# Two-layer sink-attention MLP on one core: gate high parts and some weight low parts made by GpSimd in the first layer's first run, and two start-up steps placed ahead of the last attention output

## The chip, the cores and the metric

The kernel runs on one core of a Trainium2 chip. Its time is the device time of one execution in microseconds (us). The engines are named as the profile names them: PE (TensorE, matrix products), DVE (VectorE), ACT (ScalarE), POOL (GpSimd) and SP (SyncE, which here only issues transfers). Each engine works through its own list of instructions strictly in order; semaphores make one wait for another.

## The reference, cut to what matters

```
scores = q @ k^T / 8, kept only for 4 sink keys and the last 128 keys
a = softmax(scores);  x = (a @ v) as 1536 tokens x 512
h = x @ w_in (512 x 2048);   g = h - tanh(h);              y = g @ w_out (2048 x 512)
h = y @ w_in2;               g = h * clip(h + 3, 0, 6) / 6; out = g @ w_out2
```

The weights come as 64-bit floating point numbers; everything is computed to about 32-bit accuracy.

## The kernel before

**Tiles.** The tokens are worked in three chunks of 512. A chunk needs 64 groups: 32 for the first MLP (phase 0) and 32 for the second. A group is either one 128-row slice f of the hidden layer (12 products of 128x512 into one bank `ps_h`) or its contribution to the output (12 products into four banks `ps_y`). Each weight and each activation is held as a high part and a low part (`wh`, `wl`; `xh`, `xl`; `gh`, `gl`), so a product is three matmuls: high by high, high by low, low by high. Slice f's hidden group runs about two groups ahead of its output group (`LAG`).

**Weights.** Two groups make a pair; there are 32 pairs. In the first chunk (the first run through the weights) each pair p is decoded from its 64-bit words: `w_load` (SP, 1,024 KB into `raw`), `w_scale` (ACT L107, into `dec`), `w_exponent` (DVE L118), `w_sign` (ACT L127 and L131: the low word and the sign into `r`), `w_round` (DVE L137 adds `r` into `dec`), `w_keep` (SP writes the 32-bit result to DRAM), `w_split` (POOL L151 makes `wh`, DVE L154 makes `wl`). Later chunks read the kept words and split them with ACT (L153) and DVE. `raw`, `dec`, `wh` and `wl` have four buffers each, `r` has two.

**Gates.** For each slice f of phase 0, ACT L229 takes tanh of `ps_h` into `th`, DVE L231 subtracts, ACT L232 makes the high part `gh`, DVE L233 the low part `gl`. `th` has two buffers.

**Order.** Attention for the first chunk runs first (`startup`), with the decoding of the first pairs placed between its steps by the table `WARM` (tick, stage, pair). From then on `rest` writes MLP groups and the next chunk's attention in turn. The compiler's scheduler then sorts the instructions of each engine by a model of its own, except those marked to stay in program order (the loads and scales of pairs 0 to 5, the sign steps of pairs 0 to 3). So a small edit can reorder many instructions. The last attention output of the first chunk is copied to `xh` by ACT (L562) and to `xl` by DVE (L563).

Of the kernel before, what the change touches and what calls it, by code (L numbers as in the profile page):

```python
# [8 lines left out]
F32 = mybir.dt.float32  # L9
# [19 lines left out]
GROUPS = 64  # L29
PAIRS = GROUPS // 2  # L30
# [14 lines left out]
class Mlp:  # L45
# [97 lines left out]
    def w_split(self, p):  # L143
        if p >= self.n_pairs:
            return
        nc = self.nc
        src = self.dec.pop(p).bitcast(F32) if p < PAIRS else self.raw.pop(p)
        wh = self.spl_p.tile([128, 1024], F32R, tag="wh", name="wh")
        wl = self.spl_p.tile([128, 1024], F32R, tag="wl", name="wl")
        if p < PAIRS:  # L150
            nc.gpsimd.tensor_copy(out=wh, in_=src)  # L151
        else:
            nc.scalar.copy(out=wh, in_=src)  # L153
        nc.vector.tensor_sub(out=wl, in0=src, in1=wh.bitcast(F32))  # L154
        for i in range(2):
            self.spl[2 * p + i] = tuple(
                w[:, 512 * i:512 * (i + 1)].rearrange("p (k c) -> p k c", c=128) for w in (wh, wl)
            )
# [27 lines left out]
    def step(self, s):  # L186
        c, i = divmod(s, GROUPS)
        n = self.chunks[c]
        ph, l, f = self.order[i]
        self.w_step(s // 2, s % 2)  # L190
        kd, kf = self.kd, self.kf
        if l == 0:
            ah, al = (self.xh, self.xl) if ph == 0 else (self.yh, self.yl)
            wh, wl = self.spl.pop(s)
            ps = self.ps_h.tile([128, n], F32, tag="h", name="ps_h")
            for k in range(kd):
                self.mm3(ps, wh[:, k, :], wl[:, k, :], ah[:, k, 0:n], al[:, k, 0:n], k == 0, k == kd - 1)
            self.run_late()
            self.gate(ph, f, ps, n)
            return  # L200
        if f == 0:
            self.acc = [self.ps_y.tile([128, n], F32, tag="y", name="ps_y") for _ in range(kd)]
        if f < kf - LAG:
            wh, wl = self.spl.pop(s)
            gh, gl = self.g.pop(f)
            for d in range(kd):
                self.mm3(self.acc[d], wh[:, d, :], wl[:, d, :], gh, gl, f == 0, False)
            self.run_late()
            return
        self.run_late()  # L210
        if f < kf - 1:
            return
        back = {kf - 1: s, kf - 2: s - 1, kf - 3: s - 2}
        fs = sorted(back)
        ws = {j: self.spl.pop(back[j]) for j in fs}
        gs = {j: self.g.pop(j) for j in fs}
        for d in range(kd):
            for j in fs:
                self.mm3(self.acc[d], ws[j][0][:, d, :], ws[j][1][:, d, :], *gs[j], False, j == kf - 1)
            (self.keep_y if ph == 0 else self.store)(c, d, self.acc[d], n)  # L220

    def gate(self, ph, f, ps, n):
        nc = self.nc
        th = self.ev_p.tile([128, n], F32, tag="th", name="th")
        gh = self.g_p.tile([128, n], F32R, tag="gh", name="gh")
        gl = self.g_p.tile([128, n], F32R, tag="gl", name="gl")
        self.g[f] = (gh, gl)
        if ph == 0:
            nc.scalar.activation(out=th, in_=ps, func=ACTF.Tanh)  # L229
            u = th  # L230
            nc.vector.tensor_sub(out=u, in0=ps, in1=th)  # L231
            self.late.append(lambda: nc.scalar.copy(out=gh, in_=u))  # L232
            self.late.append(lambda: nc.vector.tensor_sub(out=gl, in0=u, in1=gh.bitcast(F32)))  # L233
        else:
            nc.scalar.activation(out=th, in_=ps, func=ACTF.Relu, bias=self.three)  # L235
            u = th
            nc.vector.scalar_tensor_tensor(out=u, in0=th, scalar=6.0, in1=ps, op0=ALU.min, op1=ALU.mult)  # L237
            self.late.append(lambda: nc.scalar.activation(out=gh, in_=u, func=ACTF.Copy, scale=1.0 / 6.0))
            self.late.append(lambda: nc.vector.scalar_tensor_tensor(
                out=gl, in0=u, scalar=1.0 / 6.0, in1=gh.bitcast(F32), op0=ALU.mult, op1=ALU.subtract  # L240
            ))
# [561 lines left out]
def banded(mlp, at):  # L803
# [12 lines left out]
    (5, "scale", 0), (5, "exponent", 0), (6, "sign", 0), (7, "round", 0),  # L816
    (8, "scale", 1), (8, "exponent", 1), (8, "keep", 0), (8, "split", 0), (9, "sign", 1),
    (10, "load", 4), (10, "round", 1), (11, "keep", 1), (11, "scale", 2), (12, "exponent", 2),
    (13, "sign", 2), (13, "load", 5), (13, "scale", 3), (13, "exponent", 3), (13, "scale", 4),
)  # L820


# [93 lines left out]
```

## Time and profile before

| what | value |
|---|---|
| median of 3 runs | 670.09 us (669.36 to 671.33) |
| the profiled execution | 672.98 us, span 671.3 us |
| PE busy over the span | 637.5 us (95%) |
| DVE, ACT, POOL busy | 399.8, 361.2, 102.4 us |

The span runs from the first to the last instruction; 1.7 us of the profiled execution lie around it. Busy shares are averages over very different stretches: the first 60 us are attention, up to about 240 us weights are still decoded, and from then on PE hardly ever waits. Times below are counted from the start of the span.

### The profile page before, as it was taken

The page shows a single profiled execution, that of the slowest core. Times are in us where ns is not written, and L with a number is a line of the kernel's source. Part 1 is how long each engine was busy: PE and PEld are TensorE (multiplying, and loading weights), DVE is VectorE, ACT ScalarE, POOL GpSimd, SP SyncE. Part 2 cuts the span into 40 slices and gives each one's busy share as a digit, 9 for nine tenths or more (in the row PEclk, how much of TensorE's full clock was granted, in tenths as well). Part 3 has the DMA queues.
Part 4 walks back from the last instruction along what each step waited for, and adds up shares of the span by engine and source line. Part 5 has one row for each costly group of instructions (what it writes and reads, how often), then busy time and mean ns, then how long its engine had stood idle before and what let it go on. Part 6 is the DMA issues. An engine that isn't in the chain of part 4 may idle for free.

```text
span 671.3 us, 8169 instructions
## 1 busy us (share of the span) xinstructions
PE 637.5 (95%) x2924; PEld 489.9 (73%) x2924; DVE 399.8 (60%) x721; ACT 361.2 (54%) x608; POOL 102.4 (15%) x108
## 2 busy tenths in 40 slices
PE   2976999999999999999999999999999999999995
PEld 2654777676777787887777777778788888888884
DVE  4776899987986844465545464544354444455431
ACT  3665899788878523354544464444344443454421
POOL 1222321434332440000112020201000000000000
PEclk9999899999999999999999999999999999999999
DMA  9897999877767822332322111122133313120001
GB/s 142 271 235 192 378 417 359 286 274 256 247 225 249 263 78 84 126 109 81 102 84 106 62 63 64 62 82 109 62 126 125 126 63 125 63 89 37 0 1 67
DMA packets 38898, 98.87 MB, mean 147 GB/s; under 512 B 17857, under 2 KB 25025, under 8 KB 30657
## 3 DMA queue, kind: packets, MB, share of 16 engines
q1 hardware_dynamic: 34624, 97.22, 43.9%
q10 hardware_dynamic: 4224, 1.05, 1.1%
q8 instruction: 25, 0.41, 0.3%
q14 instruction: 25, 0.20, 0.1%
HBM read 78.33 MB, written 19.92 MB: 146 GB/s over the span
## 4 chain that ended last, share of the span: by engine, by line
PE 77%; DVE 8%; ACT 7%; issue 2%; DMA 1%; SPq 0%; POOL 0%; DVEq 0%; ACTq 0%
PE ps_h L177 12%; PE ps_y L177 12%; PE ps_h L178 12%; PE ps_h L179 12%; PE ps_y L178 11%; PE ps_y L179 11%; PE ps_a L558 4%; PE ps_a L469 3%; DVE dec L137 2%; ACT r L127 2%; DVE dec L118 2%; ACT r L131 2%; ACT dec L107 1%; PE ps_a L519 1%; DVE wl L154 1%
## 5 line engine op out<-in xcount | busy, mean ns | idle before, releaser
L178 PE MATMUL ps_y<-gl,wh 128*128 128x512 f32 x384 | 151.3, 395 | 0.0
L179 PE MATMUL ps_y<-gh,wl 128*128 128x512 f32 x384 | 149.9, 391 | 0.0
L177 PE MATMUL ps_y<-gh,wh 128*128 128x512 f32 x384 | 143.8, 403 | 2.5 <-ACT gh L232 2.5
L154 DVE TENSOR_TENSOR wl<-raw,wh 128x1024 fp32r<-128x1024 f32 x64 | 79.2, 1238 | 57.5 <-ACT wh L153 56.2
L153 ACT CAST wh<-raw 128x1024 fp32r<-128x1024 f32 x64 | 67.2, 1050 | 47.8 <-PE ps_y L178 40.2
L177 PEld LDWEIGHTS ps_y<-gh,wh 128*128 128x128 f32 x384 | 71.9, 189 | 25.3 <-issue 6.4
L178 PEld LDWEIGHTS ps_y<-gl,wh 128*128 128x128 f32 x384 | 72.2, 188 | 17.1 <-issue 2.2
L179 PEld LDWEIGHTS ps_y<-gh,wl 128*128 128x128 f32 x384 | 72.1, 188 | 15.8 <-issue 0.5
L177 PE MATMUL ps_h<-xh,wh 128*128 128x512 f32 x192 | 77.5, 406 | 6.1 <-POOL wh L151 4.4
L177 PE MATMUL ps_h<-yh,wh 128*128 128x512 f32 x192 | 76.6, 403 | 1.8 <-ACT yh L245 1.8
L179 PE MATMUL ps_h<-xh,wl 128*128 128x512 f32 x192 | 76.6, 399 | 0.0
L178 PE MATMUL ps_h<-xl,wh 128*128 128x512 f32 x192 | 76.6, 399 | 0.0
L178 PE MATMUL ps_h<-yl,wh 128*128 128x512 f32 x192 | 76.1, 397 | 0.0
L179 PE MATMUL ps_h<-yh,wl 128*128 128x512 f32 x192 | 75.9, 396 | 0.0
L235 ACT ACTIVATE th<-ps_h,three 128x512 f32<-128x512 f32 x48 | 32.8, 685 | 68.9 <-PE ps_h L179 68.7
L237 DVE SCALAR_TENSOR_TENSOR th<-th,ps_h 128x512 f32<-128x512 f32 x48 | 32.9, 685 | 55.0 <-ACT th L235 54.8
L481 ACT ACTIVATE sc<-sc,mn 128x132 f32<-128x132 f32 x96 | 38.4, 402 | 43.0 <-DVE mn L477 32.7
L469 PE MATMUL ps_a<-qk 64*128 64x264 f32 (+1 forms) x192 | 45.3, 454 | 15.0 <-DVE delta L743 9.5
L151 POOL CAST wh<-dec 128x1024 fp32r<-128x1024 f32 x32 | 43.6, 1366 | 101.9 <-PE ps_y L178 49.6
L229 ACT ACTIVATE th<-ps_h 128x512 f32<-128x512 f32 x48 | 28.6, 596 | 47.1 <-PE ps_h L179 37.5
L231 DVE TENSOR_TENSOR th<-ps_h,th 128x512 f32<-128x512 f32 x48 | 32.9, 685 | 33.6 <-ACT th L229 33.3
L177 PEld LDWEIGHTS ps_h<-xh,wh 128*128 128x128 f32 x192 | 36.3, 190 | 18.3 <-POOL wh L151 5.3
(77 smaller groups left out, 872.7 us busy)
## 6 DMA issues: line engine op xcount, KB each, us to landing
raw<-in_w_dram SPq DMA_DIRECT2D x32, 1024.0 KB
raw<-keep SPq DMA_DIRECT2D x32, 1024.0 KB
keep<-dec SPq DMA_DIRECT2D x32, 512.0 KB
out_dram<-ob SPq DMA_DIRECT2D x12, 256.0 KB
qk<-in_qkv_dram SPq DMA_DIRECT2D x8, 325.0 KB
qk<-in_qkv_dram SPq DMA_DIRECT2D x8, 260.0 KB
qk<-in_qkv_dram SPq DMA_DIRECT2D x8, 195.0 KB
v<-in_qkv_dram SPq DMA_DIRECT2D x8, 160.0 KB
```

What stands on the lines that cost most here:

```text
L151: nc.gpsimd.tensor_copy(out=wh, in_=src)
L153: nc.scalar.copy(out=wh, in_=src)
L154: nc.vector.tensor_sub(out=wl, in0=src, in1=wh.bitcast(F32))
L177: mm(out=ps, lhsT=wh, rhs=ah, start=first, stop=False)
L178: mm(out=ps, lhsT=wh, rhs=al, start=False, stop=False)
L179: mm(out=ps, lhsT=wl, rhs=ah, start=False, stop=last)
L229: nc.scalar.activation(out=th, in_=ps, func=ACTF.Tanh)
L231: nc.vector.tensor_sub(out=u, in0=ps, in1=th)
L235: nc.scalar.activation(out=th, in_=ps, func=ACTF.Relu, bias=self.three)
L237: nc.vector.scalar_tensor_tensor(out=u, in0=th, scalar=6.0, in1=ps, op0=ALU.min, op1=ALU.mult)
L469: nc.tensor.matmul(out=ps[:, 0:w], lhsT=qk[:, e, 0:128], rhs=qk[:, first:e + 1, 128:KEYS], start=True, stop=True)
L481: ins = nc.scalar.activation(out=sc, in_=sc, func=ACTF.Exp, scale=-1.0, bias=mn, accum_out=s["sm"][:, a, i:i + 1])
```

## The change

In phase 0 of the first chunk (`s < 32`, pairs 0 to 15) the high part of each gate is made by POOL and no longer by ACT: 16 casts of 128x512. Of these pairs every fourth (3, 7, 11, 15) has its weight's high part made by ACT and its low part by POOL; before, POOL made the high and DVE the low part. And the start-up table has the sign step and scale steps of pairs 2 and 3 (with one load and one exponent step) one tick earlier, so that they are written ahead of the last attention output.

```
-        if p < PAIRS:
+        if p < PAIRS // 2 and p % 4 == 3:
+            nc.scalar.copy(out=wh, in_=src)
+        elif p < PAIRS:
             nc.gpsimd.tensor_copy(out=wh, in_=src)
         else:
             nc.scalar.copy(out=wh, in_=src)
-        nc.vector.tensor_sub(out=wl, in0=src, in1=wh.bitcast(F32))
+        low = nc.gpsimd if p < PAIRS // 2 and p % 4 == 3 else nc.vector
+        low.tensor_sub(out=wl, in0=src, in1=wh.bitcast(F32))
...
+        self.decoding = s < GROUPS // 2
         self.w_step(s // 2, s % 2)
...
-            self.late.append(lambda: nc.scalar.copy(out=gh, in_=u))
+            copy = nc.gpsimd.tensor_copy if self.decoding else nc.scalar.copy
+            self.late.append(lambda: copy(out=gh, in_=u))
...
-    (13, "sign", 2), (13, "load", 5), (13, "scale", 3), (13, "exponent", 3), (13, "scale", 4),
+    (12, "sign", 2), (12, "load", 5), (12, "scale", 3), (12, "exponent", 3), (13, "scale", 4),
```

The order changes at three places that the prediction speaks of. Names carry the buffer numbers of the built program; line numbers from 150 on are up to five higher after the change.

**Place 1: ACT around the last attention output** (`xh_173` is x, `r_573` and then `r_558` the sign words of pair 2, `dec_578` and then `dec_563` the words of pair 3, `dec_581` pair 4, `th_604` and `th_638` the gates of slices 0 and 1, `r_618` and `r_672` pairs 3 and 4). Before:

```order
L562 CAST xh_173<-ps_a_558 128x512
L127 ACTIVATE r_573<-raw64_273 128x1024
L131 ACTIVATE r_573<-raw64_273 128x1024
L107 ACTIVATE dec_578<-raw64_275 128x1024
L107 ACTIVATE dec_581<-raw64_514 128x1024
L229 ACTIVATE th_604<-ps_h_591 128x512
L127 ACTIVATE r_618<-raw64_275 128x1024
L229 ACTIVATE th_638<-ps_h_623 128x512
L127 ACTIVATE r_672<-raw64_514 128x1024
L232 CAST gh_605<-th_604 128x512
```

After:

```order
L127 ACTIVATE r_558<-raw64_273 128x1024
L131 ACTIVATE r_558<-raw64_273 128x1024
L107 ACTIVATE dec_563<-raw64_275 128x1024
L567 CAST xh_173<-ps_a_566 128x512
L107 ACTIVATE dec_581<-raw64_514 128x1024
L233 ACTIVATE th_604<-ps_h_591 128x512
L127 ACTIVATE r_618<-raw64_275 128x1024
L127 ACTIVATE r_672<-raw64_514 128x1024
L233 ACTIVATE th_638<-ps_h_623 128x512
L131 ACTIVATE r_618<-raw64_275 128x1024
```

Three decode instructions stand ahead of the copy of x now, and the gate's high part has left the list.

**Place 2: POOL from the weights of pair 2 on** (`wh_645` is pair 2, `wh_697` and `wl_698` pair 3, `wh_751` pair 4, `wh_797` pair 5, `wh_856` pair 6). Before:

```order
L151 CAST wh_645<-dec_547 128x1024
L151 CAST wh_697<-dec_578 128x1024
L151 CAST wh_751<-dec_581 128x1024
L151 CAST wh_797<-dec_621 128x1024
L151 CAST wh_856<-dec_675 128x1024
```

After:

```order
L153 CAST wh_645<-dec_547 128x1024
L237 CAST gh_605<-th_604 128x512
L237 CAST gh_639<-th_638 128x512
L157 TENSOR_TENSOR wl_698<-dec_563,wh_697 128x1024
L153 CAST wh_751<-dec_581 128x1024
L237 CAST gh_667<-th_666 128x512
L237 CAST gh_717<-th_716 128x512
L153 CAST wh_797<-dec_621 128x1024
L153 CAST wh_856<-dec_675 128x1024
```

POOL's list now has gate parts and the low part of pair 3 between its casts. On PE, the four hidden groups 0 to 3 now stand wholly ahead of the first output group; before, the output group of slice 0 began after two matmuls of hidden group 3. Hidden groups 4 (pair 3) and 5 (pair 4), with two attention products between, now stand ahead of the output group of slice 2.

**Place 3: DVE up to the low part of pair 4** (`wl_752`; `dec_621`, `dec_675`, `dec_725` are pairs 5, 6 and 7). Before:

```order
L137 ISA dec_621<-dec_621,r_722 128x2048
L231 TENSOR_TENSOR th_716<-ps_h_703,th_716 128x512
L233 TENSOR_TENSOR gl_668<-th_666,gh_667 128x512
L137 ISA dec_675<-dec_675,r_776 128x2048
L154 TENSOR_TENSOR wl_752<-dec_581,wh_751 128x1024
```

After:

```order
L235 TENSOR_TENSOR th_666<-ps_h_651,th_666 128x512
L235 TENSOR_TENSOR th_716<-ps_h_703,th_716 128x512
L137 ISA dec_621<-dec_621,r_722 128x2048
L137 ISA dec_675<-dec_675,r_776 128x2048
L118 TENSOR_SCALAR dec_725<-dec_725 128x1024
L157 TENSOR_TENSOR wl_752<-dec_581,wh_751 128x1024
```

The low part of pair 4 stands behind the round of pair 6 in both, and after the change behind the exponent step of pair 7 too.

## Rows read from the trace of the kernel before

**Rows 1.** Stretch: its us; busy PE, PEld, DVE, ACT, POOL; clock, DMA share, GB/s.
```profile
66.40:71.10 4.70, 4.70 (x12) 3.69 (x13) 4.33 (x6) 3.99 (x4) 1.44 (x1) 0.52 0.87 295
...
57.80:165.00 107.20, 100.37 (x430) 73.80 (x431) 94.72 (x149) 95.36 (x139) 35.78 (x27) 0.97 0.88 317
```

**Rows 2.** All waits of PE from 66 us on: total, times, longest.
```profile
PE ps_y L177 <- ACT gh L232: 2.5, 2, 2.0
PE ps_h L177 <- ACT yh L245: 1.8, 1, 1.8
PE ps_a L469 <- DVE th L231: 0.9, 1, 0.9
```

**Rows 3.** Timeline of PE: start, us, instruction, idle before and releaser.
```profile
60.17 0.40 PE L178 MATMUL ps_h<-xl,wh 128*128 128x512 f32 x1
60.40 0.39 PE L179 MATMUL ps_h<-xh,wl 128*128 128x512 f32 x1
63.59 0.50 PE L177 MATMUL ps_h<-xh,wh 128*128 128x512 f32 x1 [2.81 <-POOL wh L151]
63.93 0.49 PE L178 MATMUL ps_h<-xl,wh 128*128 128x512 f32 x1
66.38 2.07 PE L177 MATMUL ps_y<-gh,wh 128*128 128x512 f32 x4 [1.96 <-ACT gh L232]
...
80.64 0.71 PE L469 MATMUL ps_a<-qk 64*128 64x264 f32 x2
```

**Rows 4.** Timeline of ACT, same columns.
```profile
57.77 0.59 ACT L562 CAST xh<-ps_a 128x512 fp32r<-128x512 f32 x1 [7.12 <-PE ps_a L558]
58.25 1.13 ACT L127 ACTIVATE r<-raw 128x1024 int32<-128x1024 uint32 x1
59.42 1.37 ACT L131 ACTIVATE r<-raw 128x1024 f16<-128x1024 f32 x1
60.65 2.14 ACT L107 ACTIVATE dec<-raw 128x1024 f32<-128x1024 f32 x2
62.69 0.59 ACT L229 ACTIVATE th<-ps_h 128x512 f32<-128x512 f32 x1
...
72.30 1.15 ACT L107 ACTIVATE dec<-raw 128x1024 f32<-128x1024 f32 x1 [1.91 <-DMA keep<-dec]
```

**Rows 5.** Timeline of SP's transfers (time of issue).
```profile
24.85 1.09 SPq L91 DMA_DIRECT2D raw<-in_w_dram  x2
...
58.81 4.09 SPq L449 DMA_DIRECT2D vsk<-in_vs_dram  x8
...
65.05 0.42 SPq L91 DMA_DIRECT2D raw<-in_w_dram  x1
```

**Rows 6.** One line's instructions: count, ns shortest/median/longest, first and last start.
```profile
L500 POOL TENSOR_TENSOR sc<-sc,rs x16: 1035/1040/2019, 117.4 to 433.4; 128x512 f32<-128x512 f32 x16
L151 POOL CAST wh<-dec x32: 1031/1383/2032, 34.1 to 249.6; 128x1024 fp32r<-128x1024 f32 x32
L154 DVE TENSOR_TENSOR wl<-dec,wh x32: 1164/1214/2065, 38.2 to 253.5; 128x1024 fp32r<-128x1024 f32 x32
L153 ACT CAST wh<-raw x64: 1033/1051/1077, 254.7 to 641.0; 128x1024 fp32r<-128x1024 f32 x64
L232 ACT CAST gh<-th x48: 600/621/652, 65.7 to 567.9; 128x512 fp32r<-128x512 f32 x48
L137 DVE CUSTOM_DVE_ANT_0 dec<-dec,r x32: 1209/1225/1840, 31.8 to 232.7; 128x2048 uint16<-128x2048 uint16 x32
L118 DVE TENSOR_SCALAR dec<-dec x32: 676/694/1554, 26.4 to 231.9; 128x1024 int32<-128x1024 int32 x32
L233 DVE TENSOR_TENSOR gl<-th,gh x48: 675/692/1526, 66.6 to 568.5; 128x512 fp32r<-128x512 f32 x48
```

**Rows 7.** Timeline of POOL and DVE side by side, one cast and one gate part.
```profile
68.92 1.44 POOL L151 CAST wh<-dec 128x1024 fp32r<-128x1024 f32 x1 [5.38 <-DVE dec L137]
69.38 1.53 DVE L233 TENSOR_TENSOR gl<-th,gh 128x512 fp32r<-128x512 f32 x1
```

## The prediction

> **What bounds the kernel now.** I read three views in this order: where PE waits, what it does at those places, and how full the engines that feed it are there. From 66 us to the end PE waits 5.2 us in all, and 2.0 of these are one wait at 66.38 [rows 2, 3]; after it only 3.2 us are left in 600. So an edit that relieves ACT or DVE cannot win much in the body of the run, however full they are. What there is to win lies between the last attention output (57.8 us) and about 71 us. The timeline of PE shows it as three losses [rows 3]. A matmul step is 0.23 us (60.17 to 60.40). PE ends the first three hidden groups at 60.63 and starts the fourth at 63.59: 2.96 us, for the weights of pair 2. It issues two matmuls until 64.16 and goes on at 66.38: 2.22 us, for the first gate's high part. Then it runs at a lower clock: from 66.4 to 71.1 the granted clock is 0.52, half of 2.4 GHz or hardly more, and the 12 matmuls there take 4.70 us where 12 steps of 0.232 are 2.78 us, so 1.92 us more [rows 1]. Together **7.1 us**.
>
> Behind all three stands ACT. It waits 7.12 us for the last attention output (50.65 to 57.77) with nothing to do, and then has the sign words of pair 2, two scale steps, and only at 62.69 the first tanh [rows 4]. From 57.77 on each of these follows at once on the one before.
>
> **The start-up table.** After the change three decode steps stand in that hole of 7.12 us: 1.13 + 1.37 + 1.11 = 3.6 us, so they end near 54.3 and the copy of x is not later. Their words are there: pairs 2 and 3 were asked for at 24.85 [rows 5]. Without the hole they would cost 3.6 us. Pair 2 is then rounded by 56.2 and POOL's cast done by 57.3 (1.04), before PE wants it at 60.63. The wait of 2.96 goes. What is late next is the low part of pair 2: DVE makes it behind the exponent step of pair 4, which follows ACT's scale step (58.25 to 59.36): 59.4 + 0.69 + 1.21 = 61.3. PE needs it for its third matmul at 61.1, so it loses 0.25.
>
> **The first gates.** ACT's tanh of slice 0 can start when its group ends, at 59.9, and ends at 60.5; DVE's difference follows at 61.2 to 61.9 (taken at 0.69 like the low part of the same size [rows 6]). POOL then makes the high part. No row shows a POOL cast of 128x512; its bounds are half of the shortest and of the longest cast of 128x1024, 0.52 and 1.02 [rows 6]. I take 0.6, since DVE is between two operations there; 62.5. PE wants it at 63.65, after the ten matmuls that are left of group 3. So the wait of 2.22 goes too. The low part is ready at 64.4, behind the second slice's difference; PE needs it at 64.6. With no long gap before 64 the clock should stay up, and 1.92 us with it. Output groups 0 and 1 are 24 matmuls: 69.25.
>
> **Pair 3, where the change adds a wait.** PE would want pair 3 at 69.25; before, it came there at 76.36, when pair 3 had long been made. Now ACT makes its high part and POOL its low part. I carry ACT's list on with the distances of starts in [rows 4] (L127 1.05, L131 1.23, L107 1.02, tanh 0.48): sign words of pairs 3 and 4 from 60.4 and 61.45, tanh of slice 1 at 62.5, sign of pair 3 at 63.0, scale of pair 5 at 64.2. The scale of pair 6 needs its load. SP issued it at 65.05, behind eight small transfers and four loads; now it stands behind four of the eight, near 58.81 + 2.05 = 60.9 [rows 5]. How long it takes no row tells: between 3.6 us (1,024 KB at the 295 GB/s of 66.4 to 71.1 [rows 1]) and 7.25 us (65.05 to its reader at 72.30, which waited for another transfer [rows 4]). I take 5: scale at 66.0, 0.75 us of ACT lost; at 7.25 it would be 3.0. Then sign of pair 4 at 67.0, tanh of slice 2 at 68.25, and the high part of pair 3 from 68.75 to 69.8 (1.05 [rows 6]). PE loses 0.55, issues two matmuls and waits for the low part. POOL's only comparable row is a two-input product of 128x512, 1.04 at the median and 2.02 at the longest [rows 6]; twice that is 2.08 to 4.04. DVE has little that collides there, so 2.08: from 69.85 to 71.95. **PE loses 1.65 us**, up to 3.6. DVE alone would have taken 1.21.
>
> **Pair 4.** Its high part is done by 73.1. Its low part waits in DVE's list for the rounds of pairs 5 and 6 and the exponent of pair 7. ACT, full all the while, ends the sign words of pair 6 at 74.95 (its list from 69.7: L127, tanh, L127, L131, L131), DVE rounds to 76.2, does the exponent to 76.9, or 77.7 if a cast of POOL holds it (0.69 at the median, 1.55 at the longest [rows 6]), and the low part to 78.0 or 78.8; I take 78.4. PE has ten matmuls of pair 3 (74.3), two of pair 4 and two attention products of 0.71 [rows 3] until 76.2. **It loses 2.2 us.** From there POOL and DVE are ahead: pair 5's low part would be there near 86, and PE asks for it near 88.
>
> **The sum.** Lost before 7.1; lost after 0.25 + 0.55 + 1.65 + 2.2 = 4.65; gain 2.45 us. Add nothing for the 3.2 us of later waits: 1.8 of them are the turn to the second MLP, which the change leaves. The rest of the relief has no taker: ACT loses 16 casts of 0.62 and gains 4 of 1.05 (5.7 us less in a stretch where it is busy 95.4 of 107.2), DVE loses 4 of 1.21; PE, busy 100.4 there, covers both [rows 1, 6]. If that cover went, as in a stretch where ACT ended last, these 5 us would be the gain. The profiled execution took 672.98, so 670.5 of its own kind; it was 2.9 above the median of three. From the median 670.09: **667.6 us**.
>
> **A rule that speaks against it.** POOL's cast at 68.92 took 1.44 where a lone one takes 1.03, and DVE's gate part, begun at 69.38 beside it, took 1.53 where 0.68 is the least: it ended 0.55 us after the cast did [rows 6, 7]. So one makes the other wait rather than both going slower. The Trainium skill says so of the two engines (SBUF — State Buffer, "SBUF: two separate sides"): the shared port pair is an exclusive lock, taken by a GpSimd operation or by a DVE operation with two SBUF inputs or in a two-port mode, and the other blocks. The trace agrees. By that rule every us that moves to GpSimd can be taken from DVE; this is the third rival.
>
> **Rivals.** (1) The waits for pairs 3 and 4 do not arise, because the load lands earlier and ACT and DVE run half a us ahead at each step. Then nearly all 7.1 and about 1 us of later waits go: 670.09 - 7 = 663 to 664. For it: 0.75 of ACT's time hangs on a guess. Against it: ACT's list from 60 to 75 us has no other hole. (2) It comes out even: the load takes 7.25 (2.2 us more for pairs 3 and 4), or POOL's low part is held up (1.6 to 2 us), or the clock falls again after the 2.2 us that PE idles around 70 us (1.9 us, as in [rows 1]). Each alone leaves 0 to 0.6: 669.5 to 670.5. Before, 2.96 us of idling stood ahead of the fall, so I do not expect it. (3) Slower: POOL holds DVE. Added on POOL are 16 x 0.52 + 4 x 2.08 - 4 x 1.04 = 12.5 us; taken from DVE 4.8. If all of it blocks DVE, DVE has 7.7 us more in a stretch where it is busy 94.7 of 107.2 [rows 1]: it just fits on average, but gates then come late one after the other, each PE wait of the kind of [rows 2]. If all of it reaches PE the time is 667.6 + 7.7 = 675.3. It is slower by more than the measurement can tell once over 4.5 us, more than half, reach PE; 672 to 674 then. Against it: PE wants a gate only two groups, 24 matmuls or 5.6 us, after its slice ends, and tanh and the difference read PSUM.
>
> **How the numbers follow.** No change within 0.3% (2.0 us) can be told from none in this kernel. My forecast, a gain of 1 to 4 us, has 0.52, two thirds of it beyond 2.0. Rival 1 has 0.15, rival 2 0.18, rival 3 0.15. Faster: 0.36 + 0.15 = 0.51, with a little for gains near 2: 0.53. Same: 0.16 + 0.18 = 0.34, less that: 0.31. Slower: 0.16. The range leaves out the upper half of rival 3 and the best of rival 1: 663.6 to 671.8.
>
> **What would show it.** In the new profile: PE starts hidden group 3 near 60.6 without a wait on POOL; the granted clock stays at 1.00 from 60 to 75 us; PE waits for POOL's low part of pair 3 near 70 us and for DVE's low part of pair 4 near 76 us; POOL's gate casts take 0.5 to 1.0 us and its low parts 2.1 to 3. The prediction is wrong if PE waits for gates between 90 and 165 us, if the clock falls, or if ACT's copy of x is later than 57.8.

## The result and the profile after

The changed kernel took 675.5 us (median of 4 runs, 674.04 to 676.54); before, run beside it, took 670.71 us. The ratio on record is 1.0055 (95% interval 1.0032 to 1.0078): slower by half a per cent, 3.7 us, where a gain of 2.45 us was forecast. The quotient of the two medians, 1.0071 (4.8 us), lies inside that interval; below, too, ratios on record and quotients of medians differ by up to 0.17%, and the ratios are used. The profiled execution took 676.31 us with a span of 674.6 us.

The windows of the profile after, over the stretch of [rows 1] and two short ones inside it, with the same columns:

```profile
57.80:165.00 107.20, 99.35 (x431) 72.68 (x428) 87.20 (x140) 87.24 (x120) 55.98 (x43) 0.97 0.86 301
75.65:79.06 3.41, 3.41 (x9) 2.65 (x9) 2.82 (x3) 3.41 (x4) 3.41 (x4) 0.50 1.01 419
82.48:85.89 3.41, 3.40 (x8) 2.72 (x9) 3.41 (x10) 2.80 (x4) 0.00 (x0) 0.50 0.90 296
```

DVE and ACT are 7.5 and 8.1 us less busy than in [rows 1] and POOL 20.2 us more. PE's granted clock no longer falls at 64 us; it falls to half at 75.65 and at 82.48.

All waits of PE between 57.8 and 300 us after the change (total, times, longest), to be held against [rows 2]:

```profile
PE ps_h L182 <- DVE wl L157: 2.3, 1, 2.3
PE ps_y L181 <- DVE gl L238: 2.1, 3, 0.8
PE ps_h L180 <- ACT wh L151: 1.8, 1, 1.8
PE ps_h L182 <- POOL wl L157: 1.7, 1, 1.7
PE ps_h L180 <- ACT xh L567: 0.7, 1, 0.7
```

Both waits of [rows 3] are gone. In their place stand three for the weights of pairs 3 and 4, and 2.1 us for gates. They are in PE's timeline after:

```profile
61.93 0.40 PE L180 MATMUL ps_h<-xh,wh 128*128 128x512 f32 x1
...
65.04 1.08 PE L180 MATMUL ps_y<-gh,wh 128*128 128x512 f32 x4
...
72.44 0.50 PE L180 MATMUL ps_h<-xh,wh 128*128 128x512 f32 x1 [1.77 <-ACT wh L151]
...
74.91 0.50 PE L182 MATMUL ps_h<-xh,wl 128*128 128x512 f32 x1 [1.74 <-POOL wl L157]
...
82.49 0.79 PE L182 MATMUL ps_h<-xh,wl 128*128 128x512 f32 x1 [2.32 <-DVE wl L157]
```

Hidden group 3 (61.93) and the first output group (65.04) start without a wait, as forecast. The reader should look at 82.49: pair 4's low part comes there, 4 us later than I had it. TensorE waits no longer than 2.32 us for it because it is itself late: it asks at 80.17, where I had 76.2. In e14_after_pad, a kernel below that runs the same instructions in the same order, it asks at 77.97 and waits 3.88:

```profile
81.85 0.50 PE L183 MATMUL ps_h<-xh,wl 128*128 128x512 f32 x1 [3.88 <-DVE wl L158]
```

In the trace of before that low part is done at 82.54, so the change brings pair 4 hardly earlier. The waits for gates stand at 157.24, 164.62 and 168.47.

How far PE has come is best read from the windows that begin at 0: the number behind PE's busy time counts the matmuls begun. Before:

```profile
0.00:90.00 90.00, 67.40 (x324) 47.95 (x325) 63.98 (x180) 57.99 (x118) 21.98 (x29) 0.96 0.91 255
0.00:165.00 165.00, 140.94 (x653) 101.77 (x654) 132.36 (x298) 123.09 (x223) 49.16 (x49) 0.98 0.89 283
```

After:

```profile
0.00:90.00 90.00, 65.93 (x312) 46.29 (x313) 63.38 (x182) 57.71 (x115) 28.10 (x33) 0.94 0.91 255
0.00:165.00 165.00, 139.65 (x640) 100.10 (x641) 126.32 (x290) 118.26 (x207) 69.46 (x65) 0.97 0.88 274
```

After is 12 matmuls behind at 90 us and 13 at 165 us, at 0.23 us each some 3 us. The last matmul starts at 665.43 us after and at 662.88 before. In this execution the clock was 0.50 from 24.45 to 27.86 and the copy of x at 59.06 (57.77 in [rows 4]), ahead of the changed instructions; whether that reaches the end is seen below. From the last matmul to the end of the span it is 9.2 us after and 8.4 before.

### The profile page after: what moved, and what is told of

It reads as the page before. It is cut to its first block, busy times and chain, and to the rows that moved or that the text cites. A ratio compares the mean times of both kernels' runs of the same rounds, so it can differ in the third digit from the quotient of the medians.

```text
span 674.6 us, 8166 instructions
## 1 busy us (share of the span) xinstructions
PE 639.6 (95%) x2924; PEld 491.1 (73%) x2924; DVE 395.3 (59%) x717; ACT 357.8 (53%) x596; POOL 123.9 (18%) x124
## 4 chain that ended last, share of the span: by engine, by line
PE 85%; DVE 5%; ACT 3%; issue 2%; DMA 1%; POOL 1%; POOLq 0%; ACTq 0%
PE ps_h L180 13%; PE ps_h L182 13%; PE ps_h L181 13%; PE ps_y L180 13%; PE ps_y L181 12%; PE ps_y L182 12%; PE ps_a L563 4%; PE ps_a L474 4%; DMA vsk<-in_vs_dram 1%; PE ps_a L524 1%; DVE dec L118 1%; DVE wl L157 1%; ACT r L127 1%; DVE dec L137 1%; ACT sc L486 1%
## 5 line engine op out<-in xcount | busy, mean ns | idle before, releaser
L180 PE MATMUL ps_y<-gh,wh 128*128 128x512 f32 x384 | 138.0, 399 | 0.0
L182 PE MATMUL ps_h<-xh,wl 128*128 128x512 f32 x192 | 78.2, 407 | 4.1 <-DVE wl L157 2.3
L182 PEld LDWEIGHTS ps_h<-xh,wl 128*128 128x128 f32 x192 | 36.7, 191 | 14.8 <-DVE wl L157 3.2
```

The lines of the kernel that those rows point to most:

```text
L180: mm(out=ps, lhsT=wh, rhs=ah, start=first, stop=False)
L182: mm(out=ps, lhsT=wl, rhs=ah, start=False, stop=last)
```

## The experiments

Each kernel ran beside before on the same chip; ratios are to before, with the 95% interval. "Behind" and "ahead" count matmuls by the windows above. Every edit but those of `PAD` (and before itself, run again) makes the compiler sort the lists anew from where it first acts, so a ratio prices an edit together with its new order.

**Parts alone.** e1_table has only the last hunk of the change (`WARM`), e2_gates only the gates' (`copy = nc.gpsimd.tensor_copy if self.decoding ...`), e3_split only the pairs'.

> Only the start-up table of the change; gates and weight parts as before. Theory A (the loss comes from pair 3, whose high part ACT and low part GpSimd make: PE waits 1.8 and 1.7 us for them and its clock falls twice): without that, PE goes from hidden group 3 straight on, pair 3 is there when PE comes, and at most one fall of the clock is left, so 0 to 3 us faster than before, 668 to 671. Theory B (the steps placed ahead of the last attention output delay it: it came 1.3 us later after the change): ACT's copy of x again near 59.0 us and not 57.8, 0 to 2 us slower, 671 to 673. Theory C (GpSimd's gate parts hold up VectorE): no loss, since no gate is on GpSimd here.

> Only the gates' high parts on GpSimd. Theory A: the start is as before (PE waits 2.8 us for pair 2 and 2 us for the first gate), pair 3 is made as before, so within 2 us of before, 669 to 672. Theory B: copy of x at 57.8 us as before, no loss. Theory C: GpSimd's casts of 0.6 to 1.6 us hold VectorE; gates come late after 90 us and PE waits 2 us and more for low parts of gates, so 2 to 4 us slower, 673 to 675.

> Only every fourth pair of the first half split by ACT (high) and GpSimd (low). Theory A: PE waits near 70 us for pair 3's two parts, 2 to 3.5 us more than before, and the clock falls once or twice, so 2 to 5 us slower, 672 to 676. Theory B: no loss from the start (copy of x at 57.8). Theory C: four operations of 2.4 us each on GpSimd hold VectorE a little, 0 to 2 us slower.

Measured: e1_table 1.0005 (0.9983 to 1.0027), e2_gates 1.0007 (0.9989 to 1.0025), e3_split 1.0051 (1.0036 to 1.0067). In e1_table the last copy of x is at 57.59 and hidden group 3 starts without a wait at 60.46: the moved steps do not delay x. Neither the table nor the gates alone show a loss; the split alone does.

**The split without pair 3, and none of it.** e5_no_pair3:

```
-        if p < PAIRS // 2 and p % 4 == 3:
+        if 3 < p < PAIRS // 2 and p % 4 == 3:
```

and the same for `low`; e4_table_gates leaves both lines as in before.

> The whole change, but pair 3 is split as before (GpSimd high, VectorE low); pairs 7, 11 and 15 stay as changed. Theory A: the waits of 1.8 and 1.7 us for pair 3 shrink to under 1 us together and the clock falls at most once between 60 and 90 us, so 3 to 5 us faster than the changed kernel: 670 to 673. Theory B: the copy of x is still near 59.0 us and 1.3 us of loss stay. Theory C: gates are still on GpSimd and the loss stays whole, 674 to 676.

> The whole change without the split: table and gates only. Each alone was within 0.1% of before. Theory A and rival E: no split, no cost, and the two reliefs add: before's wait for pair 2's weights (3.0 us) and for the first gate's high part (2.2 us) go, 0.995 to 0.999, with TensorE's next waits at pairs 3 and 4. Rival D: the same start as before, 0.996 to 1.000.

Measured: e5_no_pair3 1.0032 (1.0015 to 1.0050), e4_table_gates 1.0017 (1.0000 to 1.0034). Pair 3 carries part of the loss, not all. e4_table_gates begins 666 matmuls by 165 us, 13 more than before, and its last matmul is at 660.6 us, yet it is not faster (0.995 to 0.999 was forecast): 9.9 us lie behind that matmul. This led to the closing chain, below.

**The two halves of the split, and its last pair alone**, each on the kernel before. e8_high_act has only `nc.scalar.copy(out=wh, ...)` for every fourth pair, e9_low_pool only `nc.gpsimd.tensor_sub(out=wl, ...)`; e10_pair15 has both for `p == 15` alone.

> The kernel before with one half of the split alone: for every fourth pair the high part is made by ScalarE (1.04 us there) in place of GpSimd, the low part stays on VectorE. The whole split alone was 1.0051 (1.0036 to 1.0067). Theory A (the split costs where it is made, around pair 3 from 68 to 86 us): ScalarE is the fuller engine there, so this half carries about half of it: 1.002 to 1.004, with TensorE waiting 1 to 2 us for ScalarE's high part at pair 3 and 7. Rival D (the split's cost is a start-up of another kind: in the three traces with the split TensorE waits 0.3 to 0.7 us for vsk near 23 us, its clock falls to half between 18 and 28 us and the first copy of x is 1.3 to 2.1 us late; in the three without it, none of that): 1.004 to 1.005 with that fall in the trace. Rival E (GpSimd's low part of 2.4 to 3.4 us is the cost): 0.999 to 1.001.

> The kernel before with the other half of the split alone: for every fourth pair GpSimd makes the low part too (2.1 to 3.4 us), the high part stays on GpSimd (1.04 to 1.5 us). Theory A: 1.002 to 1.004, with TensorE waiting 1.5 to 3 us for GpSimd's low part of pair 3. Rival D: 1.004 to 1.005, with the wait for vsk and the fall of the clock at 18 to 28 us. Rival E: 1.005 to 1.008, since GpSimd now makes both parts of the pair one after the other.

> The kernel before with the split on the last pair of the stretch (pair 15) alone: nothing is moved ahead of about 130 us. Theory A: 0.999 to 1.001 and a start like before's. Rival D, if the start-up follows from the program holding the split at all and not from what the engines do in it: 1.003 to 1.005, with the wait for vsk and the fall of the clock at 18 to 28 us. Rival E: 1.000 to 1.002.

Measured: 1.0035 (1.0018 to 1.0051), **1.0146 (1.0117 to 1.0174)** and 1.0039 (1.0012 to 1.0066). GpSimd's low part, with the high part left on GpSimd, costs 9.8 us, more than any theory gave it. e8_high_act fits theory A by its time, but its last matmul is at 661.15 us, ahead of before, and 10.1 us lie behind it, so its time does not show that the high part on ScalarE costs anything. The windows of e9_low_pool:

```profile
0.00:90.00 90.00, 68.62 (x328) 49.36 (x329) 64.93 (x182) 59.72 (x120) 24.77 (x30) 0.94 0.93 263
0.00:165.00 165.00, 138.34 (x612) 99.48 (x613) 130.28 (x286) 121.32 (x216) 57.97 (x52) 0.95 0.88 275
```

It loses its 41 matmuls between 90 and 165 us, not at pair 3. Rival D (a start-up tied to the split) falls: e9_low_pool has the split's half and no fall of the clock before 33 us, e4_table_gates has no split and one at 24.7 us, and before_again, below, has one at 18.47 us. e10_pair15 has D's time and an early fall (19.0 to 22.4 us), but its last matmul is at 663.1 us as in before; its runs spread from 670.6 to 680.3 us, and its time is not explained.

**The clock.** e11_after_filled and e12_before_filled let PE work where it had waited; results of the added matmuls are overwritten. This is e11_after_filled; e12_before_filled has `{3: 12}`, ahead of the first output group, with `xl[:, 3]` as both operands.

```
+FILL = {6: 16, 8: 10}
...
+            for _ in range(FILL.get(s, 0)):
+                self.nc.tensor.matmul(out=ps, lhsT=ah[:, 0, 0:128], rhs=self.gk, start=True, stop=True)
```

> The changed kernel with 26 extra matmuls whose results are overwritten (16 with the second gate as operand ahead of pair 3's first group, 10 ahead of pair 4's), so that TensorE works where it waits 1.8 + 1.7 and 2.3 us in the trace of after. Nothing of the reference is left out. Theory F (the two falls to half clock between 75 and 86 us, some 3 us, are what turned the gain into a loss): the clock stays at 1.00 from 62 to 90 us and the kernel is 3 us faster than the change, 1.000 to 1.002 of before. Rival G (the weights come no earlier whatever TensorE does meanwhile, and the falls only stretch work that would wait anyway): 1.004 to 1.006 as the change itself.

> The kernel before with 12 extra matmuls (2.7 us, operands the last quarter of x's low part, results overwritten) in the 2.8 us that TensorE waits for pair 2's weights between 60.6 and 63.6 us; nothing else is changed. Theory F: the clock no longer falls at 64 us and 2 us are saved: 0.997 (0.996 to 0.998). Rival G: the first gate's high part, which comes at 66.3 us whatever TensorE does, holds the next groups as before, and the saving is under 1 us: 0.9985 to 1.001.

Measured: 1.0116 (1.0090 to 1.0143) and 1.0030 (1.0010 to 1.0049). The clock did stay up; e11_after_filled:

```profile
57.80:90.00 32.20, 31.45 (x144) 24.40 (x141) 24.67 (x27) 30.14 (x31) 14.71 (x11) 1.00 0.90 317
90.00:165.00 75.00, 70.85 (x312) 50.49 (x311) 67.21 (x116) 57.31 (x93) 39.39 (x33) 1.00 0.81 291
```

By 90 us it has begun 353 - 26 = 327 matmuls of the kernel's own, 15 more than after; by 165 us 663 - 26 = 637, 3 fewer. e12_before_filled has 346 - 12 = 334 by 90 us, 10 more than before, and 653 by 165 us, the same. PE gets ahead and then waits for weights and gates that come no earlier. The last matmul of e11_after_filled is at 664.90 (the change: 665.43, in e14_after_pad 664.86), that of e12_before_filled at 661.73, 1.2 us ahead of before. Theory F falls in both. G holds in kind, but both times lie above its ranges. For e12_before_filled the stop at the end of the program that is described below can account for it: 2.0 us, 0.3%, which before does not have. That e11_after_filled is slower than after is more than G says, and open; its profiled execution took 677.05 us, 2.4 less than its median, so the trace need not show the loss. Both kernels also have lists sorted anew, so they do not test the clock alone.

**The low parts back on VectorE, and before once more.** e13_low_dve is the change with one hunk undone:

```
-        low = nc.gpsimd if p < PAIRS // 2 and p % 4 == 3 else nc.vector
-        low.tensor_sub(out=wl, in0=src, in1=wh.bitcast(F32))
+        nc.vector.tensor_sub(out=wl, in0=src, in1=wh.bitcast(F32))
```

> The whole change with the low parts of every fourth pair left on VectorE; their high parts stay on ScalarE, the gates on GpSimd, the table as changed. Without any split it was 1.0017 (1.000 to 1.0034), with the whole split 1.0055. Theory H (GpSimd's low part, 2.4 to 3.4 us and held up behind the gates, is the part of the change that costs; with both parts on GpSimd it was 1.0146): 1.000 to 1.003. Theory A (ScalarE's high part for pair 3, for which TensorE waits 1.8 us, carries half of it): 1.003 to 1.005.

> The kernel before, once more, for a second trace of it. If the trace that the forecast rests on is typical, the last matmul starts near 662.9 us, TensorE waits 2.8 us for pair 2's weights and 2.0 us for the first gate's high part, its clock falls at 64 us, and between 90 and 300 us it waits 3.2 us. If that trace was a slow one, the three losses are there again, and what is missing is the 3.2 us of later waits: the last matmul near 660 to 661 us.

Measured: e13_low_dve **0.9988 (0.9971 to 1.0005)**, against 1.0055 for the change: the low parts on GpSimd, with the order that comes with them, cost 0.67%, 4.5 us. before_again took 671.95 us, with its last matmul at 663.0. Its waits from 57.8 us on:

```profile
PE ps_h L177 <- POOL wh L151: 2.8, 1, 2.8
PE ps_y L177 <- ACT gh L232: 2.0, 1, 2.0
PE ps_h L177 <- ACT yh L245: 1.6, 1, 1.6
PE ps_h L177 <- ACT xh L562: 0.7, 1, 0.7
```

The losses on which the forecast rests are typical. The start-up is not: here the clock was 0.50 from 18.47 to 28.71 us and the copy of x came at 59.89, 2.1 us later than in [rows 4]. So the 1.3 us that the trace of after lost there can belong to the execution, and no run shows that they cost anything at the end: with 2.1 us lost, the last matmul of before_again starts 0.1 us later than before's. Between 90 and 165 us PE does not wait at all there, where before waits 1.4 us.

**The closing chain.** In the records of SyncE, which the page counts as not busy, the chain that ends the program stands still in some kernels. Starts of its first instructions, in us:

```
before            669.90 669.98 670.04 670.11 670.18
after             670.91 672.92 673.01 673.08 673.15
e14_after_pad     670.81 670.88 670.95 671.01 671.08
e16_before_shift  668.93 669.00 669.08 669.15 671.16
```

In after an instruction transfer runs in that time; the profile's DMA view of its last 4.7 us, in 40 slices (GB/s), shows four transfers of 8 KB and nothing else:

```profile
GB/s 0 70 0 0 0 0 0 0 0 0 0 0 0 70 0 0 0 0 0 0 0 0 0 0 0 0 0 0 0 0 0 0 0 70 0 0 0 0 0 70
...
q14 instruction: 4, 0.03, 2.0%
```

SyncE has 722 instructions ahead of its closing block in before and in e2_gates, neither of which stops; 721 in after, e1_table and e4_table_gates, which stop behind the block's first instruction; 720 in e3_split and e13_low_dve, which stop behind the second. So the stop is always at the same place in SyncE's program. All kernels above have it in their times but before, e2_gates and e10_pair15 (722). The time from the last matmul to the end says the same: in all 19 traces of this document it is 9.2 to 10.3 us in the 11 with the stop and 7.2 to 8.4 in the 8 without. Three kernels change only the arm that is not run here (`PAD` is 1, 2 and 120; 723, 724 and 846 instructions):

```
 def dense(mlp, at):
+    for _ in range(PAD):
+        mlp.nc.sync.dma_start(out=mlp.keep[:, 0, 0:1], in_=mlp.three)
```

> The changed kernel with two more SyncE instructions in the dense arm, which is not run here; every instruction that runs is the same. SyncE's closing block moves from 721 to 723 instructions into its program (before: 722). Theory L (the stop of 2.0 us in the closing chain comes from where that block lies in SyncE's program): the stop is gone, the time from the last matmul to the end falls from 9.2 to 7.2 to 8.4 us, and the kernel is 1.0025 (1.001 to 1.004) of before in place of 1.0055. Rival M (the stop has to do with what the run does, not with the place): 1.004 to 1.007, stop still there.

> The change with every fourth pair's low part on VectorE (0.9988 as it stood, with the stop of 1.9 us), and four more SyncE instructions in the arm that is not run: the closing block moves from 720 to 724. Theory L: the stop is gone and it is 0.996 (0.9945 to 0.9975). Rival M: 0.997 to 1.0005 as it stood, stop still there.

> The kernel before with 124 more SyncE instructions in the arm that is not run, which puts the closing block at 846, that is 128 - 4 further; every instruction that runs is the same. Theory L, with a step of 128 instructions (8 KB): the stop of 2.0 to 2.3 us appears after the fourth instruction of the closing chain and the kernel is 1.003 (1.0015 to 1.0045). Rival M: 1.000 (0.9985 to 1.0015), no stop.

Measured: 1.0045 (1.0023 to 1.0067), **0.9961 (0.9940 to 0.9982)** and 1.0023 (1.0002 to 1.0045). The stop went in the first two and came in the third, behind the fourth instruction as forecast: theory L holds for the stop. The time of e14_after_pad lies in M's range and not in L's; its interval holds both. Of the last 3.1 us of e14_after_pad:

```profile
GB/s 26 106 0 0 0 0 0 0 0 0 0 0 0 0 0 0 0 0 0 0 0 0 0 0 0 106 0 0 0 0 0 0 0 0 0 0 0 0 0 0
...
q14 instruction: 2, 0.02, 2.1%
```

In the traces the stop is 1.9 to 2.3 us, about 0.3%. The ratios differ by 0.10, 0.23 and 0.27% (0.7 to 1.8 us), each uncertain by 0.2 to 0.3%, which agrees with that but would not show it alone. The two causes side by side:

| | stop | no stop |
|---|---|---|
| low parts on VectorE | 0.9988 | 0.9961 |
| low parts on GpSimd (the change) | 1.0055 | 1.0045 |

e15_low_dve_pad beats both kernels (by the medians it gains 0.2%). Its windows:

```profile
0.00:90.00 90.00, 69.31 (x329) 48.64 (x330) 65.35 (x186) 58.83 (x116) 26.14 (x33) 0.94 0.93 259
0.00:165.00 165.00, 143.00 (x667) 103.87 (x667) 135.01 (x302) 123.29 (x217) 63.20 (x62) 0.97 0.91 286
```

It is 14 matmuls ahead of before at 165 us (3.2 us), although its clock was at 0.50 for 10.2 us before 52 us and before's was not. Its last matmul is at 659.75, that of e13_low_dve at 660.83: 2.1 to 3.1 us ahead of before, and 4.0 to 5.7 ahead of the change's two traces.

**Which low part costs.** Both kernels are e15_low_dve_pad with a line as in e17_low_pool_7; e18_low_pool_3 has `p == 3` in it:

```
+        low = nc.gpsimd if p in (7, 11, 15) else nc.vector
```

> e15_low_dve_pad (0.9961) with the low parts of pairs 7, 11 and 15 on GpSimd, pair 3's on VectorE. Theory Q (what costs is pair 4's high part, queued behind pair 3's low part on GpSimd just where no pair is made ahead): within 0.1% of e15, 0.995 to 0.998. Theory R (each low part on GpSimd costs about the same, 1.1 to 1.4 us): 1.000 to 1.003.

> e15_low_dve_pad (0.9961) with pair 3's low part alone on GpSimd. Theory Q: the whole cost, 1.001 to 1.005, with TensorE's wait for pair 4's low part near 82 us as in after. Theory R: a quarter of it, 0.997 to 0.999.

Measured: 1.0058 (1.0034 to 1.0082) and 1.0024 (1.0008 to 1.0039). Pair 3 alone costs 0.63% (4.2 us) over e15_low_dve_pad, the three later ones 0.97% (6.5 us). Theory Q falls: pair 3 is not all. R falls too: the parts are dearer than a share each, and all four together cost 0.84% (1.0045), far less than the sum of the two. Beside pair 3's, the later three add only 0.21% (1.4 us), which is within the noise; the last matmul is at 664.57 in e18_low_pool_3 and at 664.86 in e14_after_pad. What each does is in the traces.

At pair 3 the low part delays what stands behind it in POOL's list, but that is not what PE waits for. POOL after the change:

```profile
72.48 2.38 POOL L157 TENSOR_TENSOR wl<-dec,wh 128x1024 fp32r<-128x1024 f32 x1 [6.34 <-ACT wh L151]
74.81 1.03 POOL L153 CAST wh<-dec 128x1024 fp32r<-128x1024 f32 x1
75.79 2.16 POOL L237 CAST gh<-th 128x512 fp32r<-128x512 f32 x2
77.90 3.47 POOL L153 CAST wh<-dec 128x1024 fp32r<-128x1024 f32 x2
```

The second row is pair 4's high part, done at 75.84. ACT and DVE after the change, up to pair 4's low part:

```profile
74.83 2.58 ACT L131 ACTIVATE r<-raw 128x1024 f16<-128x1024 f32 x2
```

```profile
76.24 2.78 DVE L137 CUSTOM_DVE_ANT_0 dec<-dec,r 128x2048 uint16<-128x2048 uint16 x2 [1.60 <-ACT r L131]
78.94 1.53 DVE L118 TENSOR_SCALAR dec<-dec 128x1024 int32<-128x1024 int32 x1
80.39 2.05 DVE L157 TENSOR_TENSOR wl<-dec,wh 128x1024 fp32r<-128x1024 f32 x1
```

DVE begins the round of pair 5 at 76.24, when ACT's sign words come, and by then pair 4's high part is there. Before pair 4's low part DVE still has the round of pair 6 and the exponent step of pair 7 to do. Beside POOL's casts the two rounds take 2.78 us, the exponent step 1.53 and the low part 2.05, where 2.46, 0.69 and 1.21 are usual: 2.0 us more. Pair 4 is there at 82.44.

DVE in e15_low_dve_pad, where VectorE makes pair 3's low part, and then PE:

```profile
75.63 1.23 DVE L138 CUSTOM_DVE_ANT_0 dec<-dec,r 128x2048 uint16<-128x2048 uint16 x1 [1.09 <-ACT r L132]
76.77 1.22 DVE L157 TENSOR_TENSOR wl<-dec,wh 128x1024 fp32r<-128x1024 f32 x1
```

```profile
78.04 0.50 PE L182 MATMUL ps_h<-xh,wl 128*128 128x512 f32 x1 [0.34 <-DVE wl L157]
```

Here the compiler has put pair 4's low part right behind the round of pair 5. It is done at 77.99, and PE waits 0.34 us for it. In e14_after_pad the round of pair 5 starts at 75.60, as early as here, and the low part is done at 81.79: 3.8 us later, 2.0 from steps made longer beside POOL's casts and the rest from the two steps that stand ahead. How much of this comes from pair 3's low part being on POOL, and how much from the order that the compiler chose with it, no run separates.

At the later pairs the cost in e17_low_pool_7 is read from one place of its trace, where POOL holds DVE. First POOL, then DVE, then PE:

```profile
139.49 3.14 POOL L158 TENSOR_TENSOR wl<-dec,wh 128x1024 fp32r<-128x1024 f32 x1 [1.18 <-issue]
```

```profile
140.53 3.18 DVE L158 TENSOR_TENSOR wl<-dec,wh 128x1024 fp32r<-128x1024 f32 x1
143.63 0.28 DVE L483 CUSTOM_DVE_ANT_0 sc<-ps_a,keep 128x132 f32<-128x132 f32 x1
```

```profile
143.98 0.80 PE L181 MATMUL ps_h<-xh,wh 128*128 128x512 f32 x1 [2.61 <-DVE mn L483]
```

DVE's own low part begins beside POOL's and takes 3.18 us, where 1.21 is usual; it ends 1.1 us after POOL's. The softmax step behind it is late by that much, PE waits 2.6 us for it, and the clock is 0.50 from 143.21 to 150.04. In the two traces of the change POOL also holds DVE at the later pairs (2.51 us for a low part at 93.99), but PE does not wait between 90 and 156 us.

## Why the prediction was wrong, step by step

- **The start-up table**: right. The wait of 2.96 for pair 2 is gone, and x is not late through it (57.59 in e1_table).
- **The first gates**: right. The wait of 2.22 is gone; POOL's first gate cast took 0.62 us, the median of the sixteen is 1.26 and the longest 1.61, above my 0.5 to 1.0.
- **"The clock should stay up"**: right until 75 us, then wrong: 17 matmuls at 0.50 in two stretches of 3.41 us, some 3 us in all, for which the sum has no term. In e14_after_pad there is one such stretch, behind the wait at 81.85. e11_after_filled and e12_before_filled show that a clock kept up here gives back little: 1.2 us of the last matmul's start in the second, nothing in the first, and nothing in the times. So the 1.92 us at [rows 1] were not a sure gain either.
- **Pair 3** (0.55 + 1.65): right in kind, 1.77 + 1.74 in the trace, and only the low part's 1.64 in that of e14_after_pad. POOL's low part took 2.38 us, inside my 2.08 to 4.04.
- **Pair 4, its low part at 78.4**: this is the step that failed. It was done at 82.44 (81.79 in e14_after_pad), hardly earlier than before the change (82.54). I had ACT's sign words of pair 6 at 74.95; they ended at 77.41 (76.79). I gave 0.4 us to POOL's casts holding DVE; these steps took 2.0 more. That PE's wait came out at 2.32, near my 2.2, is luck: PE was 4 us late itself, and waited 3.88 in the other trace. My "its high part is done by 73.1" was wrong too, since POOL's list has pair 3's low part ahead of it (Place 2), but at 75.84 it was done before DVE asked for it.
- **The low parts' cost on POOL**: in the sum it is pair 3's 1.65, where DVE alone would have taken 1.21, and nothing at pairs 7, 11 and 15. The runs price all four, with the order that comes with them, at 4.5 us (e13_low_dve) to 5.6 (e15_low_dve_pad against e14_after_pad), pair 3's alone at 4.2. The later three alone cost 6.5 in e17_low_pool_7, but only 1.4 beside pair 3's, in the change. This is the way of rival 3: POOL holds DVE, and what stands behind is late. The row at 140.53 shows it, 3.18 us for 1.21. The Trainium skill's rule (SBUF — State Buffer, "SBUF: two separate sides": the shared port pair is an exclusive lock for a whole instruction) is what that row shows. I gave this rival 0.15, because I spread its cost over a stretch in which DVE just fits on average; a wait arises where something urgent stands behind, not on average.
- **The signs of being wrong**: all three came. The clock fell, PE waits for gates at 157.24 and 164.62 (1.3 us), and ACT's copy of x is later than 57.8. The last is no mark of the change: x was at 57.59 in e1_table and at 59.89 in before_again.
- **What no step had**: the closing chain. The change gives SyncE one instruction fewer (721, as in e1_table), and an instruction transfer falls into its last microseconds: about 2 us in the trace, 0.7 to 1.8 by the ratios.
- **The sum**: the change with VectorE's low parts and no stop gives 0.9961, a gain of 2.6 us. That this is near my 2.45 is luck, since my sum was for a kernel with the low parts on POOL. From there to the measured loss the ratios add up because they are differences of the same numbers. The traces check it: the last matmul starts 2.0 and 2.6 us later than before with the low parts on POOL, and 2.1 and 3.1 earlier without. With the stop of 2.0 that makes a loss of 4.0 to 4.6 us, against 3.7 by the ratio and 4.8 by the medians. Rival 3 in full gave 675.3 us, and 675.5 was measured; that it is so close is luck as well, because the stop is part of it.

Open are why e11_after_filled is slower than the change, why e10_pair15 is slower at all, why pair 3's low part and the later ones cost less together than apart, and how the cost of the low parts divides between POOL's hold on DVE and the compiler's new order.

## What to carry to other kernels

When a step goes to another in-order engine, follow every list up to the operand that the busiest engine will wait for, and ask which of them ends last. Here POOL's longer list was done in time, and the low part that TensorE wanted stood two steps deep in VectorE's. Count a lock between two engines at the most urgent instruction behind it, not as a share of a stretch. Where the compiler sorts the lists anew, an edit cannot be priced apart from its order. A lower clock behind a wait need not be a loss of its own: fill the wait, and see whether the time moves. And when TensorE's last matmul and the time disagree, compare what lies behind that matmul.

## What the hardware showed that was not expected

- **A program's end depends on where its last block lies.** SyncE stopped for 1.9 to 2.3 us in its closing chain, and one 8 KB instruction transfer began within each stop, in every kernel here whose closing block had 720 or 721 instructions ahead of it (or 846), and in none with 722 to 725 (19 traces in all). 846 + 4 is 722 + 128: if one transfer carries 128 instructions in order, that is 64 bytes each (an estimate from these two numbers and the 8 KB). Adding instructions to an arm that is never run took the stop away or brought it. That SyncE waits for the transfer is read from the place and the time; no run shows it directly.
- **The start-up falls in and out of the lower clock between executions of the same kernel**: no fall before 64 us in the first trace of before, 10.2 us at 0.50 from 18.47 in the second, and x 2.1 us later. The last matmul starts at 662.88 and 663.00 all the same.
- **A two-input step of 128x1024 took 2.38 us on GpSimd at its shortest** and up to 3.38 in the change's trace (at 118.84). VectorE's low part beside it was held: in the row at 140.53 it ended 1.1 us after GpSimd's, near the 1.21 us that it takes alone.
